# A block of linear attention and feed-forward on one core: the last q tile of the first chunk around the shift products, and a new order for the side work of three chunks

## The chip, the cores and the metric

The kernel runs on one core of one Trainium2 chip. The metric is the time of one execution in microseconds (us) of the device. Engines: TensorE (PE, with PEld for its weight loads), VectorE (DVE), ScalarE (ACT), GpSimd (POOL) and SyncE (SP), which issues nearly all DMA transfers from one queue.

## The reference

One token sequence x of 2048 x 1024 (bf16) passes an adaptive layer norm, linear attention with 32 heads of 32, a second adaptive layer norm and a SwiGLU feed-forward of width 3584:

```python
mod = (_silu(c) @ w_mod).reshape(c.shape[0], 6, 1, -1)
sa, ca, ga, sb, cb, gb = ...          # six vectors of 1024
h = _layernorm(x) * (1 + ca) + sa
# _A_ref: qkv = h @ wqkv; phi(t) = where(t > 0, t + 1, exp(t)) + 1e-6; pq, pk = phi(q), phi(k)
#   kv = sum_s pk v; z = sum_s pk; o = (pq kv) / (pq z + 1e-6); result o @ wo
x = x + ga * _A_ref(h, A_wqkv, A_wo)
h = _layernorm(x) * (1 + cb) + sb
x = x + gb * _B_ref(h, ...)           # (silu(h @ w_gate) * (h @ w_up)) @ w_down
```

## The kernel before

The program is one list of operations written in order by hand. A small recording class (`_Prog`) gives each operation to its engine, and works out from the memory ranges and PSUM banks that it touches which semaphores it must wait for. Two engines that touch one PSUM bank are always ordered against each other. Every engine executes its own operations strictly in the order in which they were recorded, so the place of a line in the source is its place in its engine's queue. All recorded operations have one line, L176, in the profile; they are told apart by the names of their tiles.

**Tokens** are handled as 16 tiles of 128 (`st`), in 4 chunks of 512 (`ch`). Tile `st` is loaded to XRES, gets its mean and variance (by BN_STATS on DVE, or by `act_stats`: two passes on ACT, sum and sum of squares), a power of -1/2 on POOL (`pool_pow`, `neg_rstd`, `ln1_rstd1`, `ln1_rstd2`), is normalised on DVE (`ln1_xn`, or `ln1_xn_sum` where ACT made the sums), and is transposed by a DMA from SP into HT (`th_dma`). HT has two buffers, chunk by chunk. `th_mod(ch, dt)` then scales and shifts the 8 blocks (`dt`) of a chunk, on DVE or, for odd `dt` of chunks 2 and 3, on ACT.

**TensorE's order.** First the q phase of chunk 0 (`q_phase_chunk0`), whose matmuls are put around the products that make the scale and shift vectors (`mod_sc`) and the products of the shift with the q weights (`bias_mm`, evacuated by `bias_fin` to BIASQ). Its banks are `qb`, for output tiles nt 0 to 6; bank 0 collects scale, shift and bias columns. Output tile nt 7 is made last, in bank 0. Then come 8 K groups of chunk 0 (`k_group`) and, for chunks 1 to 3, 8 K groups and 8 Q groups each (`chunk`): 56 groups of 8 matmuls of 128x512, here called K(ch, nt) and Q(ch, nt). `next_bank` gives each group its PSUM bank: a rotation over all 8 banks for the first 40 groups, then over banks 1 to 5 for chunk 3.

**Evacuation.** `phi_evac` lets ACT write the exponential (K) or exponential and relu (Q) to one of four slots of E1 and RL; after every second group `phi_flush` lets DVE finish the pair: two minima, then for K two products that read PSUM (SCALAR_TENSOR_TENSOR pkt<-ps,e), for Q two adds from SBUF. A K bank is free after DVE's product, a Q bank after ACT's relu. For chunk 0's q tiles `q_phi`, `q_min` and `q_add` do the same with twice the slots (E1X, RLX).

**Side work.** The dictionaries `kside` (chunk 0), `s1`, `s2`, `s3` (chunks 1 to 3) hold, by group number, what is recorded right after that group: statistics and normalising of later tiles, th_mods, and the two vectors ga and, later, cb: each is a weighted sum of 8 blocks of w_mod on DVE (`macc(STG, kt)`, 8 steps in fp32), split into high and low halves (`macc_split`, which ends with a DMA transpose into MHLT) and reduced (`mod_red`, which waits for that transpose). STG is loaded by SP: 8 pieces for the first vector, one load of 2 MB (`stg1`) for the second. `th_dma`, the pk transposes of finished K tiles, wv and stg loads all share SP's queue.

After the chunks follow 16 groups of key-value products (`g_group`, `g_evac`, `kvt_mm`), the denominator (`den`, with its trip through DRAM, `rb_load`), the output projection and the feed-forward.

Of the kernel before, what the change touches and what calls it, by code (L numbers as in the profile page):

```python
# [5 lines left out]
FP32 = mybir.dt.float32  # L6
# [256 lines left out]
def bass_adaLN_cond__linear_attn_block__swiglu_ffn__prompt_kernel(  # L263
# [22 lines left out]
    with ExitStack() as es:  # L286
# [6 lines left out]
        def T(name, off, shape, dt):  # L293
            n = 1
            for s_ in shape[1:]:
                n *= s_
            assert off % 32 == 0 and off + n * mybir.dt.size(dt) <= ARENA, (name, off, shape)
            return nc.alloc_sbuf_tensor_at(name, shape, dt, offset=base + off)
# [47 lines left out]
        RL = T("rl", 188 * KB, [128, 4, 512], BF16)  # L346
        E1X = T("e1x", 192 * KB, [128, 4, 512], BF16)
        RLX = T("rlx", 196 * KB, [128, 4, 512], BF16)
        ACC = T("acc", 192 * KB, [128, D], FP32)
        MHL = T("mhl", 196 * KB, [128, 2, D], BF16)  # L350
        MHLT = T("mhlt", 192 * KB, [128, 2 * NDT, 128], BF16)
# [131 lines left out]
        def ln1_xn(st, c0=0, c1=D):  # L483
            P.dve("tensor_scalar", out=XRES[:, st, c0:c1], in0=XRES[:, st, c0:c1],
                  scalar1=MV[:, st, 0:1], scalar2=RSTD[:, st:st + 1], op0=ALU.subtract, op1=ALU.mult)
# [130 lines left out]
        def pool_pow(st):  # L616
            P.pool("tensor_tensor", out=RSTD[:, st:st + 1], in0=VE[:, st:st + 1], in1=NEGHALF[:, 0:1], op=ALU.pow)
# [78 lines left out]
        def q_part(nt, bank, dts):  # L696
            for dt in dts:
                P.pe("matmul", out=PS[:, bank, :], lhsT=WQK[:, dt, nt * 128:(nt + 1) * 128],
                     rhs=HT[:, 0, dt, :], start=(dt == 0), stop=(dt == 7))
# [3 lines left out]
        def next_bank():  # L703
            i = qk_ctr[0]
            qk_ctr[0] += 1
            return (1, 2, 3, 4, 6, 7, 5, 0)[i % 8] if i < 40 else i % 5 + 1

        def q_group(ch, nt):
            buf, bank = ch % 2, next_bank()
# [39 lines left out]
        def mod_row_b(bank, i, dst):  # L749
# [3 lines left out]
            P.wait_for("sp", [wr])  # L753
            P.dma("mdr%d" % i, dst[:], MDR[i].unsqueeze(0).to_broadcast([128, D]))

        def q_slot(nt):
            return (E1, RL) if nt < 4 else (E1X, RLX)

        def q_phi(nt, bank):
            for buf, fn_ in zip(q_slot(nt), (ACT.Exp, ACT.Relu)):  # L760
                P.act("activation", out=buf[:, nt % 4, :], in_=PS[:, bank, :], func=fn_, bias=BIASQ[:, nt:nt + 1])

        def q_min(nts):
            for nt in nts:
                e = q_slot(nt)[0][:, nt % 4, :]
                P.dve("tensor_scalar", out=e, in0=e, scalar1=1.0, scalar2=1e-6, op0=ALU.min, op1=ALU.add)

        def q_add(nts):
            for nt in nts:
                e, r = q_slot(nt)  # L770
                P.dve("tensor_tensor", out=PQT[:, nt, 0:512], in0=r[:, nt % 4, :], in1=e[:, nt % 4, :], op=ALU.add)

        def q_phase_chunk0():
            qb = [1, 2, 3, 4, 6, 7, 5]
            fin_ca(2, 2)
            for dt in (2, 3):
                h0_first(dt, "dve")
            for nts, dts in ((range(3), (0,)), (range(3), (1,)), ((3, 4, 5, 6), (0, 1))):
                for nt in nts:
                    q_part(nt, qb[nt], dts)  # L780
            for nt in range(7):
                if nt == 4:
                    mod_sc(WCA, 8, range(4, 8))
                    fin_ca(4, 4)
                    for dt in (4, 5):
                        h0_scale_only(dt)
                q_part(nt, qb[nt], (2, 3))
            act_stats(4, (0,))
            for nt in range(7):
                if nt == 6:  # L790
                    mod_sc(WSA, 0, range(6, 8))
                    fin_sa(6, 2)
                    for dt in (6, 7):
                        h0_scale(dt)
                q_part(nt, qb[nt], (4, 5))
            mod_sc(WSA, 0, range(4, 6))
            fin_sa(4, 2, True)
            for dt in (4, 5):
                h0_shift(dt)
            for nt in range(7):  # L800
                if nt == 2:
                    bias_mm((4, 5))
                q_part(nt, qb[nt], (6,))
            for nt in range(7):
                if nt == 1:
                    mod_sc(WSA, 0, range(4), range(4))
                if nt == 3:
                    mod_sc(WSA, 0, range(4), range(4, 8))
                    fin_sa(0, 4, True)
                    ln_ops[1][0]()  # L810
                if nt == 5:
                    bias_mm(range(4))
                    bias_fin()
                q_part(nt, qb[nt], (7,))
            ln_ops[1][1]()
            ln_ops[1][2]()
            ln1_rstd1(5)
            for i, dt in enumerate((4, 5, 0, 1, 2, 3, 6, 7)):
                P.pe("matmul", out=PS[:, 0, :], lhsT=WQK[:, dt, 896:1024], rhs=HT[:, 0, dt, :], start=(i == 0),
                     stop=(i == 7))  # L820
            for dt in range(4):
                h0_shift(dt)
            ln1_xn(5)
            th_dma(5)
            for nt in range(2):
                q_phi(nt, qb[nt])
            act_stats(4, (1,))
            for nt in range(2, 8):
                q_phi(nt, qb[nt] if nt < 7 else 0)
            for f in ln_ops[2]:  # L830
                f()
            act_var(4)
            pool_pow(4)
            for f in ln_ops[3]:
                f()
            ln1_rstd2(6)
            ln1_xn_sum(4)
            th_dma(4)
            q_min((0, 1))
            for st in (6, 7):  # L840
                ln1_xn(st)
                th_dma(st)
            q_add((0, 1))
            for nts in ((2, 3), (4, 5)):
                q_min(nts)
                q_add(nts)
            qk_ctr[0] = 0

        def add(d, k, f):
# [2 lines left out]
        kside = {}  # L852
        ln_ops = [ln1_stats_ops(4 + jj) for jj in range(4)]

        for c0 in (0, 256):
            for dt in range(NDT):
                add(kside, 1, lambda dt=dt, c0=c0: th_mod(1, dt, c0, c0 + 256))
        add(kside, 1, lambda: q_min((6, 7)))
        add(kside, 1, lambda: q_add((6, 7)))
        for jj, k in ((0, 3), (1, 4)):  # L860
            add(kside, k, lambda jj=jj: act_stats(10 + jj))
        q_phase_chunk0()
        for st in range(12, 16):
# [44 lines left out]
            add(s1, 2, lambda jj=jj: th_dma(8 + jj))  # L908
        for i, dt in zip([9, 9, 10, 10, 10, 11, 11, 11], range(NDT)):
            add(s1, i, lambda dt=dt: th_mod(2, dt))  # L910
        ln_half(3, s1, 8, 8, 11)
        for jj in range(4):
            add(s1, 13 + jj // 2, lambda jj=jj: ln1_xn(12 + jj))
            add(s2, 0, lambda jj=jj: th_dma(12 + jj))
        for dt in range(NDT):
            add(s2, 6 + dt, lambda dt=dt: th_mod(3, dt))
        for kt in range(NDT):
            add(s2, 4 + kt, lambda kt=kt: macc(STG, kt))
        add(s2, 13, macc_split)
        add(s2, 13, lambda: P.dma("stg1", STG[:], wmv[:, :, 4096:5120]))  # L920
        for kt in range(NDT):
            add(s3, 4 + kt, lambda kt=kt: macc(STG, kt))
        add(s3, 14, macc_split)
        add(s1, 7, lambda: P.pool("memset", ap=MROW[:], constant=0.0))
        add(s1, 7, lambda: P.pool("memset", ap=ZHL[:], constant=0.0))
        s3.setdefault(2, []).extend([mod_red, mod_row_a])
        add(s3, 12, lambda: mod_row_b(7, 0, GA_B))
        add(s3, 10, z_cols)
        chunk(1, s1)
# [326 lines left out]
```

## Time and profile before

| | |
|---|---|
| Times of the runs | 827.82, 827.47 and 1765.51 us; median 827.82 |
| The profiled execution | 828.25 us, of which the profile's span is 826.5 us |
| Granted TensorE clock | 1.000 |
| Busy in the span | PE 821.8 us, DVE 313.4 us, ACT 197.0 us, POOL 41.0 us |
| DMA | 119.32 MB, mean 144 GB/s |
| Chain that ended last | PE 98% of the span |

The busy share of an engine is its mean over stages that differ. The chain that ended last is followed back from the last instruction, at each step to what released it. A wait is the idle time of an engine ahead of an instruction and what ended it. Times in a timeline count from the start of the span; a transfer's line shows how long its issue took on SP, and the view of DMA issues tells how long after its issue it had landed.

### The profile page before, as it was taken

How to read it: one execution, taken by the hardware profiler on the slowest of the kernel's cores; microseconds unless marked ns; L12 is line 12 of the kernel's file. 1: busy time of each engine (PE TensorE's matmuls, PEld its weight loads, DVE VectorE, ACT ScalarE, POOL GpSimd, SP SyncE). 2: the span in 40 equal slices, each digit the busy share in tenths (PEclk: the TensorE clock that was granted, in tenths of full speed). 3: DMA queues.
4: the chain of work that ended last, by engine and by line, in shares of the span. 5: the costliest groups of instructions: out<-in, count | busy, mean ns of one | idle time of the engine just before them, and what ended most of it. 6: DMA issues, size and time to landing. Idle time of an engine off the chain costs nothing.

```text
span 826.5 us, 10519 instructions
## 1 busy us (share of the span) xinstructions
PE 821.8 (99%) x4322; PEld 376.3 (46%) x4322; DVE 313.4 (38%) x672; ACT 197.0 (24%) x338; POOL 41.0 (5%) x58
## 2 busy tenths in 40 slices
PE   8999999999999999999999999999999999999998
PEld 4544444444444444444444444444444444444444
DVE  5798988566945521121221112122111211221111
ACT  4658643223341111011111101111110111111011
POOL 1110000000130000020000003000000300000000
PEclk9999999999999999999999999999999999999999
DMA  9969666865697985600455580045557004553000
GB/s 314 289 144 222 167 165 147 178 177 205 155 255 241 296 249 152 169 26 26 134 152 151 151 177 25 20 133 152 151 153 182 27 19 125 152 152 87 0 26 26
DMA packets 199456, 119.32 MB, mean 144 GB/s; under 512 B 58088, under 2 KB 183152, under 8 KB 199408
## 3 DMA queue, kind: packets, MB, share of 16 engines
q1 hardware_dynamic: 199392, 118.65, 53.7%
q8 instruction: 34, 0.56, 0.3%
q14 instruction: 14, 0.11, 0.0%
q10 hardware_dynamic: 16, 0.00, 0.0%
HBM read 100.67 MB, written 4.33 MB: 127 GB/s over the span
## 4 chain that ended last, share of the span: by engine, by line
PE 98%; DMA 1%; ACT 0%; SPq 0%; DVE 0%; POOL 0%; issue 0%
PE ps L176 98%; DMA xres<-in_A_x_dram 1%; ACT ht L176 0%; SPq L176 0%; DVE xres L176 0%; POOL rstd L176 0%; DVE ve L176 0%
## 5 line engine op out<-in xcount | busy, mean ns | idle before, releaser
L176 PE MATMUL ps<-h2t,guu 128*128 128x512 bf16 x896 | 211.7, 379 | 0.0
L176 PE MATMUL ps<-h2t,gug 128*128 128x512 bf16 x896 | 211.7, 379 | 0.0
L176 DVE TENSOR_TENSOR at<-sg,ps 128x512 bf16<-128x512 bf16 x112 | 77.1, 688 | 282.7 <-PE ps L176 281.1
L176 ACT ACTIVATE sg<-ps 128x512 bf16<-128x512 f32 x112 | 66.9, 597 | 309.7 <-PE ps L176 309.7
L176 PEld LDWEIGHTS ps<-h2t,guu 128*128 128x128 bf16 x896 | 87.7, 98 | 105.7
L176 PEld LDWEIGHTS ps<-h2t,gug 128*128 128x128 bf16 x896 | 87.6, 98 | 105.5
L176 PE MATMUL ps<-wd_a,at 128*128 128x512 bf16 (+1 forms) x512 | 112.4, 377 | 0.0
L176 PE MATMUL ps<-ht,wqk 128*128 128x512 bf16 x512 | 112.1, 379 | 0.0
L176 PE MATMUL ps<-wd_b,at 128*128 128x512 bf16 (+1 forms) x384 | 85.0, 377 | 0.0
L176 DVE TENSOR_TENSOR ut<-att,gb_b 128x512 bf16<-128x512 bf16 (+1 forms) x32 | 14.6, 456 | 166.5 <-ACT att L176 166.5
L176 PEld LDWEIGHTS ps<-wd_a,at 128*128 128x128 bf16 x512 | 50.1, 98 | 59.7
L176 PEld LDWEIGHTS ps<-ht,wqk 128*128 128x128 bf16 x512 | 49.2, 98 | 58.9 <-DVE ht L176 1.0
L176 ACT ACTIVATE att<-ps 128x512 bf16<-128x512 f32 (+1 forms) x32 | 17.4, 591 | 182.1 <-PE ps L176 182.1
L176 PEld LDWEIGHTS ps<-wd_b,at 128*128 128x128 bf16 x384 | 37.6, 98 | 44.7
L176 PE MATMUL ps<-pk,xres 128*128 128x512 bf16 x256 | 56.2, 379 | 0.0
L176 PE MATMUL ps<-mw,pqt 128*128 128x512 bf16 x256 | 55.9, 379 | 0.0
L176 POOL TENSOR_SCALAR h2t<-h2t,modcol 128x512 bf16<-128x512 bf16 x32 | 26.4, 841 | 382.9 <-DMA h2t<-xn 382.9
L176 ACT ACTIVATE e<-ps 128x512 bf16<-128x512 f32 x56 | 33.3, 611 | 31.8 <-PE ps L176 16.3
L176 ACT ACTIVATE junk<-xres 128x1024 bf16<-128x1024 bf16 x26 | 27.6, 1063 | 46.5 <-DVE xres L176 34.2
L176 PEld LDWEIGHTS ps<-mw,pqt 128*128 128x128 bf16 x256 | 24.8, 98 | 30.0 <-issue 0.5
L176 PEld LDWEIGHTS ps<-pk,xres 128*128 128x128 bf16 x256 | 24.7, 98 | 29.9 <-issue 0.9
L176 DVE SCALAR_TENSOR_TENSOR xres<-ps,xres 128x512 bf16<-128x512 f32 x32 | 21.5, 688 | 11.5 <-PE ps L176 11.3
(111 smaller groups left out, 339.3 us busy)
## 6 DMA issues: line engine op xcount, KB each, us to landing
gug<-in_B_w_gate_dram SPq DMA_DIRECT2D x56, 512.0 KB, 3.9
guu<-in_B_w_up_dram SPq DMA_DIRECT2D x56, 512.0 KB, 5.2
xres<-in_A_x_dram SPq DMA_DIRECT2D x20, 256.0 KB, 4.3
stgx<-in_w_mod_dram SPq DMA_DIRECT2D x2, 2048.0 KB, 9.9
wd_a<-in_B_w_down_dram SPq DMA_DIRECT2D x4, 1024.0 KB, 7.2
out_dram<-xres SPq DMA_DIRECT2D x31, 128.0 KB, 1.7
rb<-recip_den SPq DMA_DIRECT2D x8, 384.0 KB, 8.7
xres<-in_A_x_dram SPq DMA_DIRECT2D x3, 1024.0 KB, 6.8
```

The costliest lines, as they stand in the source:

```text
L176: return getattr(e, method)(**kw)
```

## The change

- **Last q tile.** In the last pass (dt 7) nt 0 comes first; ACT then copies its bank to the new SBUF tile QRAW (fp32), and both passes of act_stats(4) follow on ACT at once. Output tile nt 7 is computed in nt 0's bank, with the two halves of the shift products after its first and its third matmul and the bias products after its fifth. `act_var(4)`, the power and the normalising of tile 4 are recorded earlier, tile 4's transpose ahead of tile 5's. The q activations run in the order QORD = 1 to 7, 0, the last from QRAW, and their slots go by that order.
- **Banks.** The rotation begins with bank 0 and ends with bank 1; groups 24 to 39 (chunk 2) get a written list.
- **Chunk 1's scaling** during K(0,0) and K(0,1): blocks 0 to 3 in two halves, blocks 4 to 7 whole (12 instructions instead of 16). Two q pairs are finished after K(0,3); before, one was finished after K(0,1) and one more in the q phase. act_stats of tiles 10 and 11 one group later.
- **Tiles 12 to 15**: statistics after groups 12 to 14 of chunk 1 (before 8, 9 and 11); normalising after group 15 and after the first group of chunk 2 (before 13 and 14); transposes recorded after the second group of chunk 2 (formerly after the first); th_mod(3) after groups 4 to 11 of chunk 2 (before 6 to 13).
- **ga and cb**: stg1 is recorded ahead of macc_split, both after group 12 of chunk 2 (before 13, in the other order); in chunk 3 the reduction goes from group 2 to group 4 and the maccs from groups 4 to 11 to groups 6 to 13.

```diff
+        QRAW = T("qraw", 202 * KB, [128, 512], FP32)
...
-            return (1, 2, 3, 4, 6, 7, 5, 0)[i % 8] if i < 40 else i % 5 + 1
+            if i < 24:
+                return (0, 2, 3, 4, 6, 7, 5, 1)[i % 8]
+            if i < 40:
+                return (0, 2, 3, 4, 6, 1, 7, 5, 0, 2, 3, 1, 4, 6, 7, 5)[i - 24]
+            return i % 5 + 1
...
+        QORD = (1, 2, 3, 4, 5, 6, 7, 0)
+
         def q_slot(nt):
-            return (E1, RL) if nt < 4 else (E1X, RLX)
+            i = QORD.index(nt)
+            bufs = (E1, RL) if i < 4 else (E1X, RLX)
+            return [t[:, i % 4, :] for t in bufs]
+
+        def q_phi(nt, src):
...
+        def q_pair(i):
+            q_min(QORD[i:i + 2])
+            q_add(QORD[i:i + 2])
...
-            act_stats(4, (0,))
...
             for nt in range(7):
-                if nt == 1:
+                q_part(nt, qb[nt], (7,))
+                if nt == 0:
+                    P.act("activation", out=QRAW[:], in_=PS[:, qb[0], :], func=ACT.Copy)
+                    act_stats(4)
+            for i, dt in enumerate(range(NDT)):
+                if i == 1:
                     mod_sc(WSA, 0, range(4), range(4))
-                if nt == 3:
+                if i == 3:
                     mod_sc(WSA, 0, range(4), range(4, 8))
+                    ln_ops[1][0]()
                     fin_sa(0, 4, True)
-                    ln_ops[1][0]()
-                if nt == 5:
+                    ln_ops[1][1]()
+                    act_var(4)
+                    pool_pow(4)
+                if i == 5:
                     bias_mm(range(4))
                     bias_fin()
-                q_part(nt, qb[nt], (7,))
-            ln_ops[1][1]()
+                P.pe("matmul", out=PS[:, qb[0], :], lhsT=WQK[:, dt, 896:1024], rhs=HT[:, 0, dt, :], start=(i == 0),
+                     stop=(i == 7))
             ln_ops[1][2]()
             ln1_rstd1(5)
-            for i, dt in enumerate((4, 5, 0, 1, 2, 3, 6, 7)):
-                P.pe("matmul", out=PS[:, 0, :], lhsT=WQK[:, dt, 896:1024], rhs=HT[:, 0, dt, :], start=(i == 0),
-                     stop=(i == 7))
             for dt in range(4):
                 h0_shift(dt)
+            ln1_xn_sum(4)
+            th_dma(4)
             ln1_xn(5)
             th_dma(5)
...
+            for nt in QORD:
+                q_phi(nt, QRAW[:] if nt == 0 else PS[:, qb[nt % 7], :])
...
-        for c0 in (0, 256):
-            for dt in range(NDT):
-                add(kside, 1, lambda dt=dt, c0=c0: th_mod(1, dt, c0, c0 + 256))
-        add(kside, 1, lambda: q_min((6, 7)))
-        add(kside, 1, lambda: q_add((6, 7)))
-        for jj, k in ((0, 3), (1, 4)):
+        for dt, c0, c1 in ([(dt, 0, 256) for dt in range(4)] + [(dt, 256, 512) for dt in range(4)]
+                           + [(dt, 0, 512) for dt in range(4, 8)]):
+            add(kside, 1, lambda dt=dt, c0=c0, c1=c1: th_mod(1, dt, c0, c1))
+        for i in (4, 6):
+            add(kside, 3, lambda i=i: q_pair(i))
+        for jj, k in ((0, 4), (1, 5)):
             add(kside, k, lambda jj=jj: act_stats(10 + jj))
...
-        ln_half(3, s1, 8, 8, 11)
+        ln_half(3, s1, 12, 12, 14)
         for jj in range(4):
-            add(s1, 13 + jj // 2, lambda jj=jj: ln1_xn(12 + jj))
-            add(s2, 0, lambda jj=jj: th_dma(12 + jj))
+            add(s1 if jj < 2 else s2, 15 if jj < 2 else 0, lambda jj=jj: ln1_xn(12 + jj))
+            add(s2, 1, lambda jj=jj: th_dma(12 + jj))
         for dt in range(NDT):
-            add(s2, 6 + dt, lambda dt=dt: th_mod(3, dt))
+            add(s2, 4 + dt, lambda dt=dt: th_mod(3, dt))
...
-        add(s2, 13, macc_split)
-        add(s2, 13, lambda: P.dma("stg1", STG[:], wmv[:, :, 4096:5120]))
+        add(s2, 12, lambda: P.dma("stg1", STG[:], wmv[:, :, 4096:5120]))
+        add(s2, 12, macc_split)
         for kt in range(NDT):
-            add(s3, 4 + kt, lambda kt=kt: macc(STG, kt))
+            add(s3, 6 + kt, lambda kt=kt: macc(STG, kt))
...
-        s3.setdefault(2, []).extend([mod_red, mod_row_a])
+        s3.setdefault(4, []).extend([mod_red, mod_row_a])
```

More of the change, by code (lines that the diff above doesn't have):

```diff
@@ L754, in mod_row_b @@
             P.dma("mdr%d" % i, dst[:], MDR[i].unsqueeze(0).to_broadcast([128, D]))
+        QORD = (1, 2, 3, 4, 5, 6, 7, 0)
         def q_slot(nt):
-            return (E1, RL) if nt < 4 else (E1X, RLX)
-        def q_phi(nt, bank):
+            i = QORD.index(nt)
+            bufs = (E1, RL) if i < 4 else (E1X, RLX)
+            return [t[:, i % 4, :] for t in bufs]
+        def q_phi(nt, src):
             for buf, fn_ in zip(q_slot(nt), (ACT.Exp, ACT.Relu)):
-                P.act("activation", out=buf[:, nt % 4, :], in_=PS[:, bank, :], func=fn_, bias=BIASQ[:, nt:nt + 1])
+                P.act("activation", out=buf, in_=src, func=fn_, bias=BIASQ[:, nt:nt + 1])
         def q_min(nts):
             for nt in nts:
-                e = q_slot(nt)[0][:, nt % 4, :]
+                e = q_slot(nt)[0]
                 P.dve("tensor_scalar", out=e, in0=e, scalar1=1.0, scalar2=1e-6, op0=ALU.min, op1=ALU.add)
@@ L770, in q_add @@
                 e, r = q_slot(nt)
-                P.dve("tensor_tensor", out=PQT[:, nt, 0:512], in0=r[:, nt % 4, :], in1=e[:, nt % 4, :], op=ALU.add)
+                P.dve("tensor_tensor", out=PQT[:, nt, 0:512], in0=r, in1=e, op=ALU.add)
+        def q_pair(i):
+            q_min(QORD[i:i + 2])
+            q_add(QORD[i:i + 2])
         def q_phase_chunk0():
@@ L804, in q_phase_chunk0 @@
             for nt in range(7):
-                if nt == 1:
+                q_part(nt, qb[nt], (7,))
[4 more added lines that the diff above has]
+                if i == 1:
                     mod_sc(WSA, 0, range(4), range(4))
-                if nt == 3:
+                if i == 3:
                     mod_sc(WSA, 0, range(4), range(4, 8))
+                    ln_ops[1][0]()
                     fin_sa(0, 4, True)
-                    ln_ops[1][0]()
-                if nt == 5:
+                    ln_ops[1][1]()
+                    act_var(4)
+                    pool_pow(4)
+                if i == 5:
                     bias_mm(range(4))
                     bias_fin()
-                q_part(nt, qb[nt], (7,))
-            ln_ops[1][1]()
+                P.pe("matmul", out=PS[:, qb[0], :], lhsT=WQK[:, dt, 896:1024], rhs=HT[:, 0, dt, :], start=(i == 0),
+                     stop=(i == 7))
             ln_ops[1][2]()
             ln1_rstd1(5)
-            for i, dt in enumerate((4, 5, 0, 1, 2, 3, 6, 7)):
-                P.pe("matmul", out=PS[:, 0, :], lhsT=WQK[:, dt, 896:1024], rhs=HT[:, 0, dt, :], start=(i == 0),
-                     stop=(i == 7))
             for dt in range(4):
                 h0_shift(dt)
+            ln1_xn_sum(4)
+            th_dma(4)
             ln1_xn(5)
             th_dma(5)
[L825 to L829, printed above, removed]
+            for nt in QORD:
+                q_phi(nt, QRAW[:] if nt == 0 else PS[:, qb[nt % 7], :])
             for f in ln_ops[2]:
                 f()
-            act_var(4)
-            pool_pow(4)
             for f in ln_ops[3]:
@@ L836, in q_phase_chunk0 @@
             ln1_rstd2(6)
-            ln1_xn_sum(4)
-            th_dma(4)
-            q_min((0, 1))
+            q_min(QORD[0:2])
             for st in (6, 7):
@@ L842, in q_phase_chunk0 @@
                 th_dma(st)
[L843 to L846, printed above, removed]
+            q_add(QORD[0:2])
+            q_pair(2)
             qk_ctr[0] = 0
```

## Prediction

> **What bounds the kernel now.** I read the page first, then the chain that ended last, then TensorE's waits, then the timelines of the stretch that the diff touches (20 to 135 us). The page:
>
> ```profile
> span 826.5 us, 10519 instructions
> PE 821.8 (99%) x4322; PEld 376.3 (46%) x4322; DVE 313.4 (38%) x672; ACT 197.0 (24%) x338; POOL 41.0 (5%) x58
> DVE  5798988566945521121221112122111211221111
> ...
> PE 98%; DMA 1%; ACT 0%; SPq 0%; DVE 0%; POOL 0%; issue 0%
> ```
>
> TensorE is the chain from 11 us to the end. DVE is only 38% busy on average, but its digits are 8 and 9 in slices 3 to 7 (41 to 145 us), exactly where the diff moves work: there DVE, in program order, decides when PSUM banks come free. Where TensorE lost anything is seen on its weight loads:
>
> ```profile
> PEld ps L176 <- DMA wsa<-in_w_mod_dram: 0.7, 2, 0.4
> PEld ps L176 <- DVE pkt L176: 0.5, 1, 0.5
> PEld ps L176 <- DVE biasq L176: 0.4, 1, 0.4
> ```
>
> A weight load is asked for early, so its idle time overstates the loss. The loss is the distance between matmul starts over the usual 216 ns. In narrow windows of the timeline I find 0.08 us at 25.9 (second half of the shift products, waiting for its weights), 0.06 at 26.8 (bias products, for the cast shift), 0.04 at 28.1 (nt 7 into bank 0, for BIASQ), 0.07 at 45 (first K group of chunk 1, for th_mod), 0.14 at 47.3 (its third K group, bank not yet emptied by DVE). After 48 us there is none from DVE, ACT or a load. So all that this change can give back is 0.39 us.
>
> **The change, part by part.** The sum is made on the profiled execution: span 826.5, its own time 828.25; the median of the runs shown is 827.82 (0.43 less). TensorE has the same 4322 matmuls.
>
> *Q phase.* The 16 shift products of the second half now start at about 27.4 (weights landed at 25.9): 0.08 gained. Between shift products and bias products there are two matmuls as before, so the 0.06 stays (BN_STATS of tile 5, 0.61 us from 27.32, is now ahead of the cast on DVE and ends at 27.93; the shift products end at 27.95). After the bias products three matmuls stand instead of two, and the next group wants bank 0: BIASQ done at 29.5, K(0,0) due at 29.8, 0.04 gained. Added: the ACT copy of nt 0 to QRAW (0.6 to 0.7 us by the ACT rows that read PSUM). It starts at 25.3 and ends at 26.0, before nt 7 wants the bank at 26.3; ACT was idle 12 us there. Without that cover it would cost its 0.7. Both passes of act_stats(4) now precede the q activations (end 28.9, so act_var and behind it BIASQ just fit); the activations end 0.2 to 0.3 later. On POOL the power for tile 4 now precedes that for tile 5, on SP transpose 4 precedes 5; both are early.
>
> *K groups of chunk 0.* Eight th_mods of 256 columns (0.257 apart) and four of 512 (0.325) take 3.36 instead of 16 x 0.257 = 4.11, and one q pair (1.07) moves behind the K(0,2), K(0,3) evacuation, where another joins it. Bank 3 is free at 45.5 (first flush done 41.1, + 3.36, two mins 0.41, the product 0.69), wanted at 47.0: 0.14 gained. The halves for dt 0 to 3 come first and all dts finish 0.4 us ahead of their matmul: 0.07 gained. DVE leaves this stretch 0.3 to 0.5 later than before. The gains so far: 0.08 + 0.04 + 0.07 + 0.14 = **0.33**.
>
> *act_stats of tiles 14 and 15, four to five groups later.* This is where it turns. ACT before:
>
> ```profile
> 61.95 0.59 ACT L176 ACTIVATE rl<-ps 128x512 bf16<-128x512 f32 x1
> 62.43 1.06 ACT L176 ACTIVATE junk<-xres 128x1024 bf16<-128x1024 bf16 x1
> ...
> 65.62 0.81 ACT L176 ACTIVATE ht<-ht,modcol 128x512 bf16<-128x512 bf16 x1
> ...
> 75.92 0.67 ACT L176 ACTIVATE rl<-ps 128x512 bf16<-128x512 f32 x1
> 76.40 1.17 ACT L176 ACTIVATE e<-ps 128x512 bf16<-128x512 f32 x2
> ```
>
> Its backlog lasts to 76.4. The first act_stats (62.43 to 64.66) sits where ACT would otherwise wait for the transposes of chunk 2 (the last lands 3.4 us after its issue at 61.24, at 64.7). Without it ACT reaches its first th_mod at about 63.8 and waits to 65.1 (DVE is 0.4 late). From there the old stretch 65.62 to 76.40 (10.78) follows plus one more act_stats (2.22): ACT ends Q(1,7) at 65.1 + 13.0 = 78.1, not 76.4.
>
> *Normalising tiles 12 to 15.* The four ln1_xn stood ahead of the Q(1,6), Q(1,7) flush; now they stand behind it, and the flush needs ACT's last relu. DVE starts them at 78.5 (before 75.06). SP:
>
> ```profile
> 75.63 5.36 SPq L176 DMA_TRANSPOSE ht<-xres  x4
> ...
> 100.69 1.91 SPq L176 DMA_TRANSPOSE mhlt<-mhl  x1
> 102.65 1.00 SPq L176 DMA_DIRECT2D stg<-in_w_mod_dram  x1
> ```
>
> First transpose at 79.1 instead of 75.63, the fourth 4.0 later, landing 3.2 after that: 86.3 (before 82.9). The wv request ahead of them on SP is long gone. th_mod(3, 0), now two groups sooner and ahead of the first macc, needs all four: DVE arrives at 83.6 (80.4 and two flushes of 1.62) and **waits 2.7 us**. Queued behind it are all maccs and K and Q flushes of chunk 2. The work from the first macc to the end of the eighth took 81.22 to 97.33 = 16.1; now 15.8 (0.6 of ACT wait gone, one th_mod of 0.3 more). So the eighth macc ends at 102.1, not 97.3. No bank is late yet: the tightest of chunk 2, K(2,5)'s, is free at 89.1 (86.3 + 0.33 + 0.67 + 0.41 + 2 x 0.61 + 0.1) and wanted at 90.2, six groups later.
>
> *stg1 ahead of macc_split.* Its load overwrites STG, so it goes out at 102.2, hardly sooner than 102.65, and the split vector's transpose is issued behind it at 104.1 (1.97 after the eighth macc). Two views of how a transpose fares with and without a load ahead of it:
>
> ```profile
> stg<-in_w_mod_dram SPq DMA_DIRECT2D x1, 2048.0 KB, 8.6
> mhlt<-mhl SPq DMA_TRANSPOSE x1, 4.4
> ...
> wd_b<-in_B_w_down_dram SPq DMA_DIRECT2D x1, 1024.0 KB, 8.2
> ...
> mhlt<-mhl SPq DMA_TRANSPOSE x1, 5.1
> ```
>
> The lower pair is a later transpose, issued at 277.7, behind a wd_b load issued at 272.75: it landed 1.9 us after that load (282.8 against 280.9). stg1 lands between 102.2 + 7.3 (a 256 KB load alone takes 2.65, each further one 0.66) and 102.2 + 8.6 (the row above, with a transpose ahead of it): I take 110.3. So mhlt lands at **112.2**, bounds 111.4 to 112.8. In the Trainium skill, "DMA: Bandwidth & Descriptors", section "Queues, rings and completion order", descriptors of one queue are consumed in ring order on each engine while completion isn't strictly first in, first out; the pair at 277.7 agrees with the ring order, a transpose that completed early would give the first rival below.
>
> *mod_red from group 2 to group 4 of chunk 3, maccs from group 4 to 6.* DVE before:
>
> ```profile
> 105.09 2.29 DVE L176 TENSOR_REDUCE red<-mhlt 128x8 f32<-128x2048 bf16 x1
> 107.41 0.17 DVE L176 CAST mrow<-red 128x8 bf16<-128x8 f32 x1
> 107.49 0.49 DVE L176 TENSOR_SCALAR e<-e 128x512 bf16<-128x512 bf16 x2
> 107.90 0.68 DVE L176 SCALAR_TENSOR_TENSOR pkt<-ps,e 128x512 bf16<-128x512 f32 x1
> 108.51 0.08 DVE L176 DVE_READ_ACCUMULATOR pkt<-ps,e 128x1 f32 x1
> ```
>
> From the reduce's start to the bank's release: 108.59 - 105.09 + 0.05 = 3.55. Behind the reduce now stands the flush of K(3,4), K(3,5). K(3,4)'s bank 5 is wanted five groups later by Q(3,1): before at 114.76 (from ACT's exponentials of Q(3,0) and Q(3,1)), now at 114.43. Free at 112.2 + 3.55 = 115.75: **a new stall of 1.3** (0.5 to 1.9 with the bounds). Nothing later undoes it, since TensorE has no idle time to absorb it. The new bank order is otherwise free: every other bank has at least 0.6.
>
> *Behind it.* The maccs end some 3 us later, hence the second mhlt, den's reciprocal and the rb loads. The first product that needs them is kvt_mm(0): its G block was ready about 2.9 before TensorE came; TensorE is 1.0 later itself, DVE about 3.7, so 0.2 is left: taken as no cost, at most 0.5.
>
> Sum: -0.33 + 1.3 = **+1.0**. Profiled execution 829.25; median 827.8 + 1.0 = **828.8**.
>
> **Rivals.**
> - *No new stall: it only gains.* The mark is the reduce's start: before 110.9 the bank is in time. It could start there if DVE's wait at 86.3 is 1.3 us shorter (ACT's backlog smaller than my 78.1) or if the transpose lands 4.4 after its issue at 104.1, at 108.5, as it did with nothing ahead. Then 827.8 - 0.33 = 827.5. Against it: the row at 277.7, and every step of ACT's queue is a row. For it: mod_red was given two groups (3.5 us) more. The Trainium skill's same page, section "Rules for kernel authors", says to issue a DMA early and wait late; by that rule this is the outcome, with stg1 no longer waited for (2.1 us of DVE at 111.3).
> - *Two stalls.* DVE's lateness is carried past chunk 3, and kvt_mm(0), with 0.2 left by my count, waits for its G block too. With mhlt at 113.0 the first stall is 113.0 + 3.55 - 114.43 = 2.1 and kvt_mm(0)'s 0.5: 827.8 + 2.6 - 0.33 = 830.1. For it: DVE has no idle time from 86 to 134. Against it: a later TensorE gives back what it waits.
> - *The change doesn't do what it says*: "requested ahead of its turn" gains 0.45 us of issue time at most, by the chain above; this is part of my forecast, not a time of its own.
>
> **How the numbers follow.** Forecast 0.58, only a gain 0.27, two stalls 0.13, something unseen 0.02. The likeliest: 828.8, its own range 828.0 to 829.4. The range for 8 in 10 takes in the gain (827.5, less 0.2 of scatter) and most of the two stalls: 827.3 to 830.6. Over or under 2% means 16.6 us, about what a measurement of this kernel can tell from no change; TensorE's idle time is under 5 us and no wait above reaches 3, so faster 0.01, within 0.97, slower 0.02.
>
> **What would show it.** Right: ACT's last relu of chunk 1 near 78; transposes 12 to 15 issued from 79; a DVE wait of 2 to 3 us for ht<-xres near 84 to 86; stg requested near 102 with mhlt behind it, landing past 111; one weight-load wait on DVE pkt near 115 and none near 47; no wsa or biasq wait. Wrong: mhlt landing before 110.9, or DVE reaching the eighth macc before 99. Then the time is below 827.8.

## The result, and the profile after

The changed kernel takes **829.95 us** (median of 8 runs, 829.82 to 831.16); the kernel before, beside it, 827.85. The ratio is 1.0026, interval 1.0017 to 1.0036: slower by 2.1 us, which is under the 2% bound and over what chance explains. One run of the kernel before, at 1765.51 us, was disturbed and is left out of the ratio. The profiled execution took 830.43 us, of which 828.3 are the span (the kernel before: 828.25 and 826.5).

The page, and TensorE's weight-load waits of the changed kernel (us in total, how often, the longest):

```profile
span 828.3 us, 10440 instructions
PE 816.8 (99%) x4243; PEld 375.9 (45%) x4322; DVE 311.5 (38%) x668; ACT 196.9 (24%) x339; POOL 40.8 (5%) x58
PE 85%; DVE 6%; DMA 3%; ACT 2%; SPq 2%; issue 1%; POOL 0%; ACTq 0%; DVEq 0%
```

```profile
PEld ps L176 <- DVE pkt L176: 2.6, 2, 1.7
...
PEld ps L176 <- DMA wsa<-in_w_mod_dram: 0.7, 1, 0.7
PEld ps L176 <- DMA wqk<-in_A_wqkv_dram: 0.6, 1, 0.6
```

TensorE did the same work (4322 weight loads; some 80 matmul records are missing), but the chain that ended last no longer runs through TensorE alone: 6% of it goes through DVE and 3% through DMA. These shares tell where the chain runs, not what was lost. The wait on BIASQ is gone, and of the waits for wsa one of the two. Instead of one wait for DVE's pkt there are two, five times as long in sum (2.6 against 0.5). The timeline of TensorE shows where:

```profile
104.68 3.19 PE L176 MATMUL ps<-ht,wqk 128*128 128x512 bf16 x14
108.20 7.08 PE L176 MATMUL ps<-ht,wqk 128*128 128x512 bf16 x31 [0.34 <-DVE pkt L176]
116.52 3.84 PE L176 MATMUL ps<-ht,wqk 128*128 128x512 bf16 x17 [1.24 <-DVE pkt L176]
```

By the distance between starts over the usual 216 ns these are **0.50 us** at 107.5 (K(3,5) wants bank 1, which K(3,0) held) and **1.40 us** at 114.9 (Q(3,1) wants bank 5, which K(3,4) held). From 30 to 135 us nothing else is lost to a wait for DVE or ACT; the waits at 45 and 47 are gone. The first product with pk starts at 128.67 (before 126.84) and the last matmul at 825.88 (before 824.08), so after chunk 3 nothing more is lost and nothing won back.

How DVE came to be late can be followed in the order of the prediction's steps. This is ACT, with its new wait for the transposes of chunk 2 and its statistics behind the scalings:

```profile
65.67 0.81 ACT L176 ACTIVATE ht<-ht,modcol 128x512 bf16<-128x512 bf16 x1 [1.14 <-DMA ht<-xres]
...
78.24 0.61 ACT L176 ACTIVATE rl<-ps 128x512 bf16<-128x512 f32 x1
78.72 1.11 ACT L176 ACTIVATE e<-ps 128x512 bf16<-128x512 f32 x2
```

These are DMA issues on SP; the column after the start is how long the issue took:

```profile
79.89 5.35 SPq L176 DMA_TRANSPOSE ht<-xres  x4
...
103.08 0.38 SPq L176 DMA_DIRECT2D stg<-in_w_mod_dram  x1
105.01 5.89 SPq L176 DMA_TRANSPOSE mhlt<-mhl  x1
```

And this is DVE, which between its two waits, from 87.19 to 110.38, has no idle time to speak of:

```profile
87.19 0.41 DVE L176 TENSOR_SCALAR ht<-ht,modcol 128x512 bf16<-128x512 bf16 x1 [2.75 <-DMA ht<-xres]
...
101.72 1.27 DVE L176 SCALAR_TENSOR_TENSOR acc<-stg,siluf,acc 128x1024 f32<-128x1024 bf16 x1
...
107.45 0.68 DVE L176 SCALAR_TENSOR_TENSOR pkt<-ps,e 128x512 bf16<-128x512 f32 x1
108.06 0.08 DVE L176 DVE_READ_ACCUMULATOR pkt<-ps,e 128x1 f32 x1
...
112.97 2.29 DVE L176 TENSOR_REDUCE red<-mhlt 128x8 f32<-128x2048 bf16 x1 [2.58 <-DMA mhlt<-mhl]
...
115.77 0.68 DVE L176 SCALAR_TENSOR_TENSOR pkt<-ps,e 128x512 bf16<-128x512 f32 x1
116.38 0.08 DVE L176 DVE_READ_ACCUMULATOR pkt<-ps,e 128x1 f32 x1
```

The two accumulator reads end at 108.14 and 116.46, and TensorE starts again at 108.20 and 116.52. stg1 landed at 111.19, 8.11 after its issue, and the split vector's transpose at 112.94, 1.75 behind it. In the kernel before, the product that freed K(3,0)'s bank stood here, and K(3,5) started at 107.79, so that the bank had 3.4 us of room:

```profile
103.71 0.68 DVE L176 SCALAR_TENSOR_TENSOR pkt<-ps,e 128x512 bf16<-128x512 f32 x1
```

The two waits are not independent. The second ends when DVE frees bank 5, at 116.52, and DVE's dates up to there were fixed before TensorE first stopped: its eighth macc ended at 103.00 and the load was issued at 103.08. Without the 0.50 at 107 TensorE would have come to bank 5 earlier by as much, and the second wait would have been 1.90 (an estimate from these dates). So the 0.50 adds nothing to the total while the later wait is there; it shows when the later wait is taken away.

### The profile page after: what moved, and what is told of

It reads as the page before. It is cut to its first block, busy times and chain, and to the rows that moved or that the text cites. A ratio compares the mean times of both kernels' runs of the same rounds, so it can differ in the third digit from the quotient of the medians.

```text
span 828.3 us, 10440 instructions
## 1 busy us (share of the span) xinstructions
PE 816.8 (99%) x4243; PEld 375.9 (45%) x4322; DVE 311.5 (38%) x668; ACT 196.9 (24%) x339; POOL 40.8 (5%) x58
## 4 chain that ended last, share of the span: by engine, by line
PE 85%; DVE 6%; DMA 3%; ACT 2%; SPq 2%; issue 1%; POOL 0%; ACTq 0%; DVEq 0%
PE ps L176 85%; SPq L176 2%; DVE pkt L176 2%; DVE acc L176 1%; DMA xres<-in_A_x_dram 1%; DMA mhlt<-mhl 1%; DMA ht<-xres 1%; ACT rl L176 1%; DVE e L176 1%; ACT junk L176 1%; ACT e L176 1%; DVE xres L176 1%; DVE ht L176 0%; DVE pqt L176 0%; DVE stats L176 0%
```

## The experiments

Theory A: each of TensorE's waits is a date at which DVE or ACT delivers, less the date at which TensorE wants. DVE waits 2.75 us for the transposes of tiles 12 to 15, so all that it does in chunks 2 and 3 is late (the 0.50). The load ahead of the split vector's transpose delays the reduce further, and a flush stands behind that reduce (the 1.40). The rivals say that it is one of these alone, or that the edits of chunk 0 cost the time.

Times are medians. The first four kernels ran beside one another, with the kernel before at 827.91; the last four on another chip, with the kernel before at 828.21. The kernel with stg1 on GpSimd's queue has 5 runs, the changed kernel 8, the others 11. "Waits" is what TensorE lost between 30 and 135 us in the profiled execution, by the distance of starts; "span" is that execution's, "median span" that of all runs.

| kernel | us | ratio to before (interval) | waits of TensorE: where, us | span | median span |
|---|---|---|---|---|---|
| before | 827.85 | | 45: 0.07; 47: 0.14 | 826.5 | 826.2, second chip 826.5 |
| changed | 829.95 | 1.0026 (1.0017 to 1.0036) | 107: 0.50; 115: 1.40 | 828.3 | 828.0 |
| split first | 828.40 | 1.0006 (0.9997 to 1.0015) | 107: 0.54 | 826.6 | 826.7 |
| reduce behind the flush | 829.00 | 1.0012 (1.0003 to 1.0021) | 107: 0.55 | 826.7 | 827.0 |
| tiles 12 to 15 back | 828.64 | 1.0009 (1.0000 to 1.0018) | 73: 0.73 | 827.4 | 826.9 |
| chunk 0's edits alone | 828.67 | 1.0007 (0.9998 to 1.0016) | 72: 0.78 | 827.0 | 826.9 |
| late edits alone | 829.37 | 1.0014 (1.0005 to 1.0023) | 45, 46: 0.16; 114: 1.20 | 827.2 | 827.3 |
| th_mod(3) back | 828.11 | 0.9998 (0.9989 to 1.0007) | 44: 0.18; 100: 0.08 | 826.1 | 826.1 |
| stg1 on GpSimd's queue | 831.58 | 1.0045 (1.0032 to 1.0057) | 107: 0.91; 115: 2.73 | 829.8 | 829.8 |
| one statistic later | 827.68 | 0.9994 (0.9985 to 1.0003) | none | 826.1 | 825.9 |

The waits are read within one trace; the medians scatter as much as these effects, for two reasons.

- The start-up. The span less its waits lies between 825.8 and 826.6 in the ten profiled executions. In the eight kernels that share the new chunk 0, TensorE comes to the last matmul ahead of the second bias products at 27.70 (th_mod(3) back) to 28.50 (tiles back), and the span less its waits follows, 798.1 to 798.2 us behind it in all eight. The two kernels with the old chunk 0 differ by 0.5 us in the same way.
- Time outside the span. The time of a run less its span is 1.74 to 1.76 us (median) in the kernel before and in four of the others, but 1.97 in the changed kernel, with the reduce behind the flush and with the late edits alone, 1.91 with the tiles back and 2.08 with th_mod(3) back. No record shows what those 0.2 to 0.3 us are.

So the verdicts below go by the waits first. By the median span, too, every experiment lies within 0.5 us of what its waits say.

### Split first

```
-        add(s2, 12, lambda: P.dma("stg1", STG[:], wmv[:, :, 4096:5120]))
         add(s2, 12, macc_split)
+        add(s2, 12, lambda: P.dma("stg1", STG[:], wmv[:, :, 4096:5120]))
```

> The changed kernel with one order undone: the late vector is split and its transpose issued first, and the stg1 load goes out behind it (in group 12 of chunk 2, as the change has it). Theory A (the 1.40 us stall at 114.9 us comes from the transpose landing behind the 2 MB load, and the reduce behind it): the transpose, issued at about 105.0, lands about 4.4 us later, at 109.4 instead of 112.94; the reduce starts at 110.4, when the flush of K(3,2) and K(3,3) is done; K(3,4)'s bank 5 is free at 110.4 + 3.55 = 113.95, before 115.1 where it is wanted. The 1.40 us go; the 0.50 us stall at 107.5 stays, because nothing ahead of it is changed. stg1 lands about 115.6 and DVE waits about 1 us for it, with nothing urgent behind it. Time 829.95 - 1.4 = 828.5. Rival B (the reduce is late anyway, since DVE as a whole is late; the load ahead of the transpose is no matter): the reduce still starts at about 113 and the time stays at 829.9. Rival C (stg1, now later, becomes the wait): the stall at 114.9 goes and one of more than 1 us comes near 118 to 122; 829.5 or more.

The measured time is 828.40. These are SP's issues, and TensorE:

```profile
104.72 1.93 SPq L176 DMA_TRANSPOSE mhlt<-mhl  x1
106.69 1.00 SPq L176 DMA_DIRECT2D stg<-in_w_mod_dram  x1
```

```profile
107.91 12.26 PE L176 MATMUL ps<-ht,wqk 128*128 128x512 bf16 x54 [0.37 <-DVE pkt L176]
```

The transpose was issued no earlier, but its issue took 1.93 instead of 5.89 us and it landed 4.37 later, at 109.09. The wait at 115 is gone, the one at 107 stays (0.54), and stg1, landing at 115.63, holds TensorE up nowhere (DVE waited 1.55 for it). This is as theory A said; rivals B and C fall.

### Reduce behind the flush

```
-        s3.setdefault(4, []).extend([mod_red, mod_row_a])
+        s3.setdefault(5, []).extend([mod_red, mod_row_a])
```

> The changed kernel with the reduce of the split vector moved from group 4 to group 5 of chunk 3, behind the flush of K(3,4) and K(3,5); the load still goes out ahead of the transpose. Theory A (a flush queued on DVE behind an instruction that waits for a late landing): the transpose still lands at 112.9 and DVE still waits for it, but K(3,4) and K(3,5) have been flushed by about 112.2, so the 1.40 us stall at 114.9 goes; the 0.50 us stall at 107.5 stays: 828.5. The next flush behind the reduce, K(3,6) and K(3,7), is done by about 117.5, before its bank is wanted at 118.5. Rival B (lateness of DVE, not the order): DVE has the same work to do and the stall moves to the next bank: near 116 to 118.5, 829.5 to 829.9.

The transpose still landed at 112.79, and DVE still waited for it, but only with the flush done:

```profile
111.45 0.69 DVE L176 SCALAR_TENSOR_TENSOR pkt<-ps,e 128x512 bf16<-128x512 f32 x1
112.07 0.08 DVE L176 DVE_READ_ACCUMULATOR pkt<-ps,e 128x1 f32 x1
112.82 2.29 DVE L176 TENSOR_REDUCE red<-mhlt 128x8 f32<-128x2048 bf16 x1 [0.67 <-DMA mhlt<-mhl]
```

The 1.40 us are gone here too, with no wait after 108, so rival B falls. The late landing costs TensorE something only through what is queued behind the instruction that waits for it. The median, 829.0, is 0.5 above the expected 828.5 and 0.6 above that of the split first, while its profiled execution (828.45, span 826.7) is not. By the waits the two kernels are equal; of the 0.6, 0.2 lies outside the span and 0.3 between the median spans, where nothing in the two traces explains it.

### Tiles 12 to 15 back

```
-        ln_half(3, s1, 12, 12, 14)
+        ln_half(3, s1, 8, 8, 11)
...
-            add(s1 if jj < 2 else s2, 15 if jj < 2 else 0, lambda jj=jj: ln1_xn(12 + jj))
-            add(s2, 1, lambda jj=jj: th_dma(12 + jj))
+            add(s1, 13 + jj // 2, lambda jj=jj: ln1_xn(12 + jj))
+            add(s2, 0, lambda jj=jj: th_dma(12 + jj))
```

> The changed kernel with statistics, normalising and transposes of tiles 12 to 15 put back to where they were before the change; the earlier th_mod(3), the load ahead of the split, the later reduce and all edits of chunk 0 stay. Theory A (the 2.75 us that DVE waits for the transposes of chunk 3 make everything of chunk 2 and 3 late): DVE's wait near 84 goes, the eighth macc ends before 99.5, stg1 is requested by 99.5 and lands by 108, the split vector by 109.5; both stalls (0.50 at 107.5 and 1.40 at 114.9) go: 829.95 - 1.9 = 828.0. It may not reach the full 827.5, because ACT's statistics of tiles 14 and 15 then stand ahead of its scaling of chunk 2 again: the last of those ended at 72.69 before, the eighth matmul of K(2,0) started at 73.1, and the change brings TensorE 0.2 to 0.3 forward and ACT 0.3 to 0.7 back, so up to 0.5 us of new wait at 73. Rival B (the load ahead of the transpose costs by itself, the tiles' move is harmless): the 0.50 us go, the 1.40 us stay: 829.4. Rival C (the edits of chunk 0 cost the time): no gain, 829.9.

TensorE has one wait for ACT in chunk 2 and runs through the stretch of the two late waits:

```profile
73.22 3.03 PE L176 MATMUL ps<-ht,wqk 128*128 128x512 bf16 x12 [0.30 <-ACT ht L176]
...
99.83 20.45 PE L176 MATMUL ps<-ht,wqk 128*128 128x512 bf16 x93
```

Both late waits are gone, although the load still goes out ahead of the transpose (issues at 99.96 and 101.89, landings at 107.92 and 109.66): three microseconds earlier, the same order delays no matmul. Rivals B and C fall as explanations of the late waits. In their place came 0.47 and 0.26 us at 72.5 and 73.4, for ACT. The time, 828.64, is 0.6 above the expected 828.0. The wait of 0.73, where at most 0.5 was allowed for, makes 0.2 of it; another 0.15 lies outside the span, and the rest is not accounted for.

### Chunk 0's edits alone

The four late hunks of the diff are undone; all edits up to `act_stats(10 + jj)` stay.

> Only the edits of chunk 0 (raw copy of the first q tile, its order, the bank list, th_mod(1) in mixed widths, the q pairs moved, statistics of tiles 10 and 11 one group later); everything from chunk 1 on stands as before the change. Theory A: the edits of chunk 0 cost nothing and the late edits cost 1.9: 827.85 - 0.33 = 827.5 if nothing takes the place of the waits removed, 827.8 to 828.0 if ACT's last scaling of chunk 2 is then late at 73 as said for the run with the tiles put back. Rival C (the early edits cost, by the start being 0.2 us later in the changed kernel's profile, or by ACT's raw copy): 828.3 or more, and the first K group starts later than 29.9.

The measured time is 828.67, not 827.5 to 828.0. K(0,0) started at 29.84 (before 29.88), so rival C's mark is absent, though its time came: the edits of chunk 0 do cost, but at 72 to 73 and not at the start. These are TensorE's waits, and ACT ahead of them:

```profile
PEld ps L176 <- ACT ht L176: 1.3, 2, 0.8
```

```profile
67.16 1.05 ACT L176 ACTIVATE junk<-xres 128x1024 bf16<-128x1024 bf16 x1
68.10 0.20 ACT L176 ACTIVATION_READ_ACCUMULATOR junk<-xres 128x1 f32 x1
68.33 1.06 ACT L176 ACTIVATE junk<-xres 128x1024 bf16<-128x1024 bf16 x1
69.29 0.19 ACT L176 ACTIVATION_READ_ACCUMULATOR junk<-xres 128x1 f32 x1
...
72.00 1.52 ACT L176 ACTIVATE ht<-ht,modcol 128x512 bf16<-128x512 bf16 x2
```

ACT scales the fifth and seventh slice of chunk 2 (dt 5 and 7) only now, behind the statistics of tile 15; K(2,0) wants them at 72.36 and, 0.43 later, at 72.79, and gets them at 72.83 and 73.52. In the kernel before, the same two scalings are

```profile
71.17 1.52 ACT L176 ACTIVATE ht<-ht,modcol 128x512 bf16<-128x512 bf16 x2
```

They end at 72.00 and 72.69, with the matmuls at 72.61 and 73.04: the second has 0.35 us of room. The edits of chunk 0 use it up, because they make DVE late, and ACT with it: ACT's last wait ahead of the scalings, for DVE's pkt, ends at 62.29 instead of 61.45, 0.84 late, while TensorE comes 0.25 earlier. So the move of the statistics is no mere loss: it removes 0.78 us of waiting that the early edits bring, and then costs 1.90 elsewhere.

### Late edits alone

The complement: chunk 0 as before, the late hunks as changed.

> The complement of the run with the edits of chunk 0 alone: chunk 0 as before the change, and all edits of chunks 1 to 3 as in the changed kernel. Theory A (one clock: each stall is a date at which DVE delivers less a date at which TensorE wants): without the edits of chunk 0 DVE is 0.7 to 1.0 us earlier from 41 us on and TensorE 0.2 later, so the 0.50 us stall at 107.5 goes and the 1.40 us one becomes 0.6 to 0.9; no wait at 73, because ACT's statistics stand behind its scaling: 827.9 + 0.75 = 828.6. Rival D (the two halves of the change simply add up): 829.95 - (828.67 - 827.91) = 829.2, with both stalls of the changed kernel in the trace at their old lengths.

The measured time is 829.37. The waits at 45 and 46 are those of the kernel before, the one at 107 is absent, and one remains in chunk 3:

```profile
104.67 9.66 PE L176 MATMUL ps<-ht,wqk 128*128 128x512 bf16 x43
115.36 4.92 PE L176 MATMUL ps<-ht,wqk 128*128 128x512 bf16 x21 [1.03 <-DVE pkt L176]
```

It is 1.20 us, more than the 0.6 to 0.9 expected: in this execution TensorE was 0.5 us ahead of the kernel before from the start (44.5 against 45.0 at its first wait), and gives that back here. Rival D, that the halves add up, falls in the trace: neither half alone has the 0.50 at 107. The time, 829.37 against 828.6 and 829.2, does not tell them apart.

### th_mod(3) back

```
-            add(s2, 4 + dt, lambda dt=dt: th_mod(3, dt))
+            add(s2, 6 + dt, lambda dt=dt: th_mod(3, dt))
```

> The changed kernel with one edit undone: th_mod(3, dt) after group 6 + dt of chunk 2 again instead of 4 + dt. Theory A (DVE's 2.75 us of waiting for the transposes of tiles 12 to 15 is what makes everything later late): two maccs and the flush of K(2,4) and K(2,5) fill that wait (0.66 + 1.62 + 1.2 us), DVE comes to th_mod(3, 0) at about 87.9 when the last transpose has landed; the eighth macc ends at about 100.3 instead of 103.0, stg1 is requested at 100.4, the split vector lands at 110.2, bank 5 is free at 114.0: both stalls go, 829.95 - 1.9 = 828.0. Rival B (the load ahead of the transpose costs whatever the date): the 0.50 us go, 1 us or more stays at 115: 829.3.

The measured time is 828.11 for the expected 828.0: theory A's time, by one number changed; rival B falls. With the tiles as late as in the changed kernel (last transpose landed at 86.96), DVE does two maccs and a flush first and arrives when they have landed:

```profile
84.22 0.75 DVE L176 TENSOR_SCALAR acc<-stg,siluf 128x1024 f32<-128x1024 bf16 x1
...
86.50 1.28 DVE L176 SCALAR_TENSOR_TENSOR acc<-stg,siluf,acc 128x1024 f32<-128x1024 bf16 x1
87.70 0.41 DVE L176 TENSOR_SCALAR ht<-ht,modcol 128x512 bf16<-128x512 bf16 x1
```

stg1 goes out at 99.80, the transpose lands at 109.56, and no bank is late. The price of the old place is 0.08 us at 99.8, where TensorE just waits for a th_mod of chunk 3.

### stg1 on GpSimd's queue

```
-        add(s2, 12, lambda: P.dma("stg1", STG[:], wmv[:, :, 4096:5120]))
+        add(s2, 12, lambda: P.dma("stg1", STG[:], wmv[:, :, 4096:5120], queue="pool"))
```

> The changed kernel with the stg1 load requested on GpSimd's queue instead of SyncE's, at the same place in the program; the transpose of the split vector stays on SyncE's queue. Theory A1 (the transpose waits in the order of its own queue): it lands about 4.4 us after its issue at 105.0, at 109.4, the 1.40 us go and the 0.50 stay: 828.5. Theory A2 (the 16 DMA engines are shared and the load's packets hold the transpose up from whatever queue): it lands at 112 or later and the time stays at 829.9; between the two if they take turns.

The measured time is 831.58, the slowest of all. TensorE's second wait has grown to 2.73, and of the issues (KB, median us from issue to landing) the transpose took 9.3 us:

```profile
118.04 2.33 PE L176 MATMUL ps<-ht,wqk 128*128 128x512 bf16 x10 [2.56 <-DVE pkt L176]
```

```profile
stg<-in_w_mod_dram POOLq DMA_DIRECT2D x1, 2048.0 KB, 9.0
mhlt<-mhl SPq DMA_TRANSPOSE x1, 9.3
```

The transpose is alone on its queue and issued 1.36 us behind the load, yet it lands at 114.47, 1.58 behind the load's landing at 112.89. So theory A1 fails where it was put to the test: being on another queue does not free the transpose. The packets show how the two orders differ. In the changed kernel, with both on SP's queue, none of the transpose's packets (256 bytes) ran between 105 and 110 us, while the load's (2 KB) did:

```profile
DMA packets 930, 1.90 MB, mean 381 GB/s; under 512 B 0, under 2 KB 0, under 8 KB 930
```

With the load on GpSimd's queue (q0, packets of 4 KB), the transpose's packets (q1) take turns with it, about one for one, as here between 109.5 and 111.5 us (packets, MB, share of the engines' time):

```profile
q0 software_dynamic: 177, 0.72, 94.8%
q1 hardware_dynamic: 166, 0.04, 9.9%
```

Turns of one packet each give the transpose little, since its packets are 16 times smaller. And up to 109.4 none of them had run, 4.2 us after the issue; in the run with the split first they were running 1.5 us after theirs. What held the first ones back is not shown. So it is the engines that are shared, as A2 said. In these two runs the queue decided only whether the transpose came behind the load or in turns with it; either way it landed 1.6 to 1.75 us after the load.

A2's time, 829.9, was wrong. The load was requested 0.77 later than in the changed kernel and took 0.93 longer, and the transpose landed 1.53 later, which is most of the growth from 1.40 to 2.73. The growth at 107, from 0.50 to 0.91, is not the queue's doing: TensorE came there 0.2 earlier, from its start-up, and DVE 0.2 later, as it already was when the load was requested (its eighth macc ended at 103.19 instead of 103.00). In the Trainium skill, "Trainium Kernel Development and Optimization", section "Key Constraints", queues of several issuing engines run on the same 16 DMA engines and interleave, and another queue saves issue time alone. This run agrees on the sharing, with its 177 and 166 packets; of issue time nothing was saved for the transpose, which was issued at 105.21 (changed kernel 105.01) and took 6.25 us to issue.

### One statistic later

Chunk 0's edits alone, and:

```
-                    add(d, k_act + jj, lambda jj=jj: act_stats(st + 2 + jj))
+                    add(d, k_act + 3 * jj, lambda jj=jj: act_stats(st + 2 + jj))
...
-        ln_half(3, s1, 8, 8, 11)
+        ln_half(3, s1, 8, 8, 12)
```

> The edits of chunk 0 alone, and of the later ones only this: ACT's statistics of tile 15 move from group 9 to group 11 of chunk 1, behind its last scaling of chunk 2 (those of tile 14 stay at group 8, where ACT waits for transposes anyway), and the two tiles' variances on DVE from group 11 to 12. Theory A: the last scalings end at about 69.9 instead of 73.6, so the two waits at 72.1 and 73.1 (0.78 us together in the run with chunk 0 alone) go; tiles 12 to 15 are normalised and transposed as early as before (first transpose issued by 76.8), so no stall comes at 107 or 115. No wait of TensorE for ACT or DVE is left between 30 and 135 us: 828.67 - 0.78 = 827.9, and 827.91 - 0.33 = 827.6 by the other count; the kernel before should be matched or beaten by up to 0.3. Rival (ACT passes the delay on): ACT's activations of chunk 1 end at 78 or later instead of 76.7 and a bank is late near 75 to 80: 828.3 or more.

The measured time is 827.68, and TensorE has no wait between 30 and 135 us. ACT's scalings come ahead of the statistics of tile 15, and those of tile 14 fill the time in which it would wait for transposes:

```profile
69.70 1.54 ACT L176 ACTIVATE ht<-ht,modcol 128x512 bf16<-128x512 bf16 x2
71.11 1.08 ACT L176 ACTIVATE junk<-xres 128x1024 bf16<-128x1024 bf16 x1
```

ACT still ends chunk 1 early enough that tiles 12 to 15 go out from 76.39 (before 75.63, changed 79.89), so nothing downstream moves, and the rival falls. It beats the changed kernel (each as a ratio to the kernel before that ran beside it: 0.9994 against 1.0026, and the intervals don't touch); against the kernel before the median is 0.5 lower, but the interval (0.9985 to 1.0003) still holds no difference. What the trace shows for certain is the 0.21 us of waits at 45 and 47 that it no longer has.

## Why the prediction was right, and where it was not

The forecast was 828.8, slower by 1.0, with a chain of named dates; measured is 829.95, slower by 2.1. The direction, the chain of causes behind the main wait and the forecast that it stays under 2% are right. The size is half: 829.95 lies above the forecast's own range of 828.0 to 829.4 and within the wide one of 827.3 to 830.6. The first rival's mark, a reduce that starts before 110.9, did not come (112.97).

- **The four gains, 0.33.** The 0.21 at 45 and 47 is gone in the trace. The waits behind the 0.12 at the start are gone too, but what that was worth can't be seen in the time: it is smaller than the 0.8 us by which the start-up scatters. The bias products' 0.06 stayed, as said.
- **"The activations end 0.2 to 0.3 later": mis-sized.** They ended 0.72 later (39.07 against 38.35): 0.3 is tile 4 landing at 26.89 instead of 26.59 in this execution, 0.09 the two activations from QRAW, which take 0.61 to 0.62 from start to start instead of 0.57. Then "DVE leaves this stretch 0.3 to 0.5 later" became 1.0 (57.64 against 56.63 at the first normalising of chunk 2).
- **The dates of tiles 12 to 15** carried that error and little else: ACT's wait ended at 65.67 (forecast 65.1), its last relu at 78.85 (78.1), the first transpose went at 79.89 (79.1), the last landed at 87.06 (86.3), DVE waited 2.75 (2.7), the eighth macc ended at 103.0 (102.1).
- **"Every other bank has at least 0.6": this step failed.** By the forecast's own dates K(3,0)'s bank would have been free at about 107.3 and wanted four groups of 1.73 ahead of 114.43, at 107.5: 0.2, not 0.6. With DVE 0.9 and TensorE 0.2 later it was 0.50 late. The run with late edits alone has DVE earlier and no wait there.
- **stg1 ahead of the split: the right reason, and a number that is right by luck.** Requested at 103.08, the load landed 8.11 later (forecast 8.1), the transpose 1.75 behind it (1.9), and the bank came free 3.55 after the reduce's start (3.55). That this is what makes the wait is shown by the runs with the split first and with the reduce behind the flush. But the wait of 1.40 (forecast 1.3) is the difference of two late dates: the bank was free at 116.52 instead of 115.75, and TensorE wanted it at 115.13 instead of 114.43, of which 0.50 is the wait at 107 that was not foreseen. The total is what DVE's lateness makes of the forecast: 1.3, and 0.77 for the later bank, less 0.2 for TensorE's later start, is 1.9.
- **The ring order**, which the forecast gave as the reason for the transpose's late landing, is what the packets of the changed kernel show, but the delay doesn't need it: from another queue the transpose came 1.58 behind the load all the same.
- **kvt_mm(0)**: no cost, right. The rival "two stalls" had 830.1, the nearest time of all, but with its second stall at kvt_mm(0). Two there were, the other one at 107.
- **What was not weighed:** the statistics of tiles 14 and 15 were counted as loss alone. The edits of chunk 0 without that move lose 0.78 at 73. The forecast looked for what a later instruction delays, and not for what the instructions ahead of it had been delaying.

The sum as measured, in the span: 0.50 + 1.40 - 0.21 = 1.7, against 1.8 between the spans of the two profiled executions. Of the 2.1 between the medians, a further 0.2 lies outside the span.

## What to carry to other kernels

On an in-order engine price a moved instruction twice: by what it now waits for, and by what is queued behind it; the reduce one group later, or th_mod two groups later, took away 1.4 or 1.9 us of waiting for 0.08 at most. When everything on an engine slips by a microsecond, list the slack of every consumer again, also that of banks which the edit doesn't touch: here a bank with 3.4 us of room and a scaling with 0.35 came late, without a change to the bank's place or the scaling's. Don't add up waits one behind the other without asking whether the later one would have taken up the earlier. Put a small transfer that someone waits for ahead of a large one that nobody needs yet; another queue was no substitute in the one run that tried it.

## What was not expected of the hardware

A transpose behind a 2 MB load also holds SP itself: its issue took 5.89 us (1.93 with nothing ahead), and 6.25 when the load was on GpSimd's queue. The pk transpose behind it was issued only at 110.95 and 111.50. The same 2 MB load ran in 2 KB packets and took 8.11 us from SP's queue, and ran in 4 KB packets and took 9.04 from GpSimd's, in one execution each. An activation with the FP32 tile in SBUF took 0.61 to 0.62 us from start to start, against 0.57 for the same one from PSUM.
